# Casts of k and q issued half a pair earlier, first row-maximum pieces in score tiles, and low parts of channel weights shared by GpSimd and VectorE

## The chip, the cores and the metric

One core of a Trainium2 chip runs the whole program. The metric is device time in microseconds (us), the median of several executions. The profile's times count from the start of the profiled span.

## What is computed

The reference runs three stages one after the other. Only the first and the last are touched.

```python
q_pool = q.reshape(B, H, S // 2, 2, D).mean(axis=3)          # 4 x 8 heads, 576 x 64
scores = scale * np.matmul(q_pool, k.transpose(0, 1, 3, 2))  # 576 x 1152
attn = np.exp(scores - np.max(scores, axis=-1, keepdims=True))
attn = attn / (np.sum(attn, axis=-1, keepdims=True) + 1e-09)
x = np.matmul(attn, v)                                       # -> 4 x 576 x 512
...
u, v = relu(x @ w_in), halves                                # gated MLP
x = (u * (w_spatial @ norm(v) + b_spatial)) @ w_out
...
u = x + (x^T @ U @ V)^T                                      # channel MLP
out = u + np.maximum(u @ w_ch1, 0.0) @ w_ch2                 # 512 -> 2048 -> 512
```

The weights of both MLPs arrive as 64-bit floats and are turned into 32-bit ones on the core, then into a rounded high part and a low part (the rest), so that three rounded matmuls stand in for an exact one.

## The kernel before

**Attention.** The 32 heads are worked in 16 pairs; a pair fills the 128 partitions with two heads. A pair has two halves of query columns, 256 and 320 wide, and 9 chunks of 128 keys for each, so 18 chunks, taken in 9 groups of two (`r` is the group's number in its pair, 0 to 8, `i` the group's number in all). A group's work on TensorE is `scores` (L214), `less` (L223, which takes off the row maximum), then `pv` of the group before (L250). ScalarE turns scores into exponentials (`expo`, L234) and GpSimd adds them up (L239). Score tiles come from `ps_s`, which has two buffers.

The row maximum is found beforehand from rounded copies of q and k, in pieces (`piece`, L166 for two heads at once, L163 for the last query columns): one or two matmuls into a PSUM tile `r`, then a reduction on VectorE (L174 or L178) and, after the last piece of a row block, a small minimum (L176, or L184 twice for the last columns). The tile `r` comes from `ring`, which has one buffer, so a piece waits for the reduction of the one before. In each group `some()` issues up to the next piece that is due; by the end of group r = 1 all pieces of the pair itself are done, and the first piece of the next pair stands at the start of group r = 2. `to_rows` turns the maxima of a half into a row (L195, L200 on TensorE, copied by ScalarE at L201 and L206).

The rounded copies are made by ScalarE: `round_k` (L141, one cast of 128x1152) and `round_q` (L130, 128x512, and L135 twice, 64x64). They write one of two buffers (`krs`, `qrs`, `qds`), by the parity of the pair. Before, `round_q(j + 1)` stands at the end of group r = 0 of pair j and `round_k(j + 1)` at the end of r = 1, each behind the exponentials of that group. q itself is pooled by GpSimd (`pool_q`, L124) at the end of r = 4, two pairs ahead.

In the first two groups of the program, one more piece stands behind the scores of each chunk (`if i < 2: some()`), all of them in the one ring buffer.

**Weights.** `Weights.tick` moves one unit of weights (128 x 512 for the channel MLP) through a row of phases, one a tick: two ScalarE passes over the raw words (L493, L494), a clamp and a shift on VectorE (L498, L500), an integer add on GpSimd (L502), a merge on VectorE (L504), the high part on ScalarE (L514) and the low part, a subtraction `do_lo` (L519). Ticks of the gated MLP's weights fall into the attention, one unit every six groups; those of the channel MLP's first ten units fall into the last batch of the gated MLP (table `CFG["END"]`), the other 22 into the first items of the channel MLP. Units alternate: `w1` of block m, `w2` of block m. Before, all 32 low parts run on VectorE.

**Around it.** In the gated MLP's last batch VectorE multiplies (L836), ScalarE and GpSimd split the product (L394, L395), TensorE makes `py` (L860), VectorE takes its low part (L395, tile `yh`), and TensorE's `pU` (L846) needs that. The channel MLP then begins with transposes (L1052), `ph` (L1060) and `py` (L1074).

The order on each engine is the order of the code (the schedule is manual); engines run their queues in order.

Of the kernel before, what the change touches and what calls it, by code (L numbers as in the profile page):

```python
# [10 lines left out]
F32 = mybir.dt.float32  # L11
F32R = mybir.dt.float32r
ACTF = mybir.ActivationFunctionType
ALU = mybir.AluOpType
AX = mybir.AxisListType
# [16 lines left out]
def attention(tc, idf, q, k, v, xs, rounded, also):  # L32
# [13 lines left out]
    nc = tc.nc  # L46
    NP, D, _, _, T = q.shape
# [15 lines left out]
    with ExitStack() as ctx, ExitStack() as sco:  # L63
# [62 lines left out]
        def round_q(j, c0=0, c1=T):  # L126
            s = st[j]
            if "qr" not in s:
                s["qr"] = qrs[j % 2]
            nc.scalar.copy(s["qr"][:, c0:min(c1, 512)], s["q"][:, c0:min(c1, 512)])  # L130
            if c1 == T:
                s["qd"] = qds[j % 2]
                for e in range(2):
                    p = slice(D * e, D * e + D)
                    nc.scalar.copy(s["qd"][p, D * e:D * e + D], s["q"][p, 512:T])  # L135

        def round_k(j, c0=0, c1=S):
            s = st[j]
            if "kr" not in s:
                s["kr"] = krs[j % 2]  # L140
            nc.scalar.copy(s["kr"][:, c0:c1], s["k"][:, c0:c1])  # L141
# [12 lines left out]
        done = [0]  # L154

        def piece(r=None):
            u, c, i, at = pieces[done[0]]
            done[0] += 1
            s, q0 = st[u // 2], HALF[u % 2][2][c]
            r = ring("r") if r is None else r  # L160
            for h, k0 in enumerate(at):
                if c == 2:
                    nc.tensor.matmul(r[:, h, 0:PW], s["qd"], s["kr"][:, k0:k0 + PW], start=True, stop=True)  # L163
                for e in range(2 if c < 2 else 0):
                    p = slice(D * e, D * e + D)
                    nc.tensor.matmul(  # L166
                        r[:, e, 0:PW], s["qr"][p, q0:q0 + 128], s["kr"][p, k0:k0 + PW], start=True, stop=True
                    )
            if i == 0:
                jobs[u]["m"] = ld.tile([128, 2, NPC], F32, tag="m", name="m", bufs=4)  # L170
            m = jobs[u]["m"]
            t = tops[u // 2 % 2][c + 2 * (u % 2)].rearrange("p (e d) -> p e d", e=2)[:, :, 0]
            if c < 2:
                nc.vector.tensor_reduce(out=m[:, :, i], in_=r[:, :, 0:PW], axis=AX.X, op=ALU.max, negate=True)  # L174
                if i == NPC - 1:
                    nc.vector.tensor_reduce(out=t, in_=m, axis=AX.X, op=ALU.min)  # L176
            else:
                nc.vector.tensor_reduce(  # L178
                    out=m[:, 0, i:i + 1], in_=r[:, 0:len(at), 0:PW], axis=AX.XY, op=ALU.max, negate=True
                )  # L180
                if i:
                    for e in range(2):
                        p = slice(D * e, D * e + D)
                        nc.vector.tensor_tensor(out=t[p, e:e + 1], in0=m[p, 0, 0:1], in1=m[p, 0, 1:2], op=ALU.min)  # L184

        def to_rows(u):

            h = u % 2
            n = HALF[h][1]
            t = jobs[u]["top"] = ld.tile([128, NMAX], F32R, tag="toprow", name="toprow")  # L190
            rs = ring("tr")
            for c in range(2):
                for i in range(2):
                    p = slice(64 * i, 64 * i + 64)
                    nc.tensor.matmul(  # L195
                        rs[:, i, 64 * c:64 * c + 64], tops[u // 2 % 2][c + 2 * h][p], idr[p],
                        start=True, stop=True,
                    )
            if h:
                nc.tensor.matmul(rs[:, 0, 128:192], tops[u // 2 % 2][4], idr, start=True, stop=True)  # L200
            nc.scalar.copy(  # L201
                t[:, 0:256].rearrange("p (c i x) -> p i c x", c=2, i=2),
                rs[:, :, 0:128].rearrange("p i (c x) -> p i c x", c=2),
            )
            if h:
                nc.scalar.copy(t[:, 256:n], rs[:, 0, 128:192])  # L206
# [100 lines left out]
        pool_q(1, nc.gpsimd)  # L307
        busy(6)
        to_rows(0)
        chunks = [(u, c) for u in range(NJ) for c in range(KC)]  # L310
        groups = [chunks[i:i + G] for i in range(0, len(chunks), G)]
        PG = 2 * KC // G
# [11 lines left out]
        for i, group in enumerate(groups):  # L324
            j, r = divmod(i, PG)
            if r == 0:
                if j + 2 < NP:
                    load_k(j + 2)
                    load_q(j + 2)
                if j + 1 < NP:  # L330
                    load_v(j + 1)

            end = min(upto[1] + AHEAD + upto[2] * (i + 1) // PG, upto[NJ])

            def some():
                if done[0] < end:
                    piece()

            new = [u for u, c in (groups[i + 1] if i + 1 < len(groups) else ()) if c == 0]
            for u in new:  # L340
                while done[0] < upto[u + 1]:
                    piece()
                to_rows(u)
            if not new:
                some()
            for x in smalls.pop((i, 0), ()):
                x()
            for u, c in group:
                scores(u, c)
                if i < 2:  # L350
                    some()
            last = jobs[group[-1][0]]["s", group[-1][1]]
            for u, c in group:
                less(u, c)
                expo(u, c)
            some()
            for x in smalls.pop((i, 1), ()):
                x()
            if i + 1 == len(groups):
                break  # L360
            for x in before:
                pv(*x)
            before = group

            if i in sums_at:
                sums(sums_at[i], last, NMAX)
            also(i)
            if r == 4 and j + 2 < NP:
                pool_q(j + 2, nc.gpsimd)
            if r == 0 and j + 1 < NP:  # L370
                round_q(j + 1)
            if r == 1 and j + 1 < NP:
                round_k(j + 1)
        sco.close()
        for x in before:
            pv(*x)
# [607 lines left out]
def channel_mlp(tc, ctx, idf, w1, w2, us, out):  # L984
# [4 lines left out]
    nc = tc.nc  # L989
# [27 lines left out]
    for m in range(KM):  # L1017
        src = w1[:, 128 * m:128 * m + 128].rearrange("(k p) f -> p k f", p=128)
        units.append(
            ([(slice(None), src)], 128, (KD, 128))  # L1020
            + parts(
                nc, lambda m=m: [w1s[m][:, 0]], lambda m=m: [w1s[m][:, 1]],
                lambda st: st.rearrange("p (k f) -> p k f", k=KD), nc.vector,
            )
        )
        units.append(
            ([(slice(None), w2[128 * m:128 * m + 128])], 128, (DM,))
            + parts(nc, lambda m=m: [w2s[m][:, 0]], lambda m=m: [w2s[m][:, 1]], eng=nc.vector)
        )

    un, ut, py = {}, {}, {}
# [180 lines left out]
```

## Time and profile before

| | |
|---|---|
| median of 3 runs | 1183.41 us (1182.99 to 1185.17) |
| the profiled execution | 1184.43 us, its span 1182.7 us |
| attention, to the first matmul of the gated MLP | about 515 us |
| gated MLP | about 515 to 757 us |
| channel MLP | about 757 to 1183 us |

Engines' busy time is an average over three stages of different make; the places where TensorE stands still are what the change can act on. In a timeline row the first column is the start, the second the time from the first start to the last end, and the bracket gives the idle time of that engine before it and what ended it.

### The profile page before, as it was taken

Reading aid. Unit: us, or ns where it says so; the run is one execution under the profiler, and the core shown is the slowest. Engines: PE = TensorE matmul, PEld = TensorE weight load, DVE = VectorE, ACT = ScalarE, POOL = GpSimd, SP = SyncE. Lnnn points to the kernel's source line nnn. Section 1 sums busy time; section 2 is a strip of 40 time slices with the busy share of each in tenths; the row PEclk is TensorE's granted clock in tenths of the full one; section 3 lists DMA queues with packets and bytes.
Section 4 is the critical chain, followed back from the end, with each engine's and each line's share of the span. In section 5 each row is a group of like instructions: output and inputs, shape, how many; then the busy total and the mean of one; then the engine's idle time right before and its main releaser. Section 6 shows DMA issues by size and latency. Waiting matters only on the chain.

```text
span 1182.7 us, 18287 instructions
## 1 busy us (share of the span) xinstructions
PE 1135.9 (96%) x7242; PEld 887.0 (75%) x7242; DVE 616.7 (52%) x967; ACT 446.6 (38%) x877; POOL 566.4 (48%) x467
## 2 busy tenths in 40 slices
PE   7999999999999999999999999799999999999998
PEld 5655556655655555669898988689999999999997
DVE  4576777766787777544333336888822112121211
ACT  2455555455545555444333334555411111111110
POOL 2789999988889988843242436353300000000000
PEclk7899999999999999999999999899999999999999
DMA  7122333333334320011020106343202001010000
GB/s 213 27 82 82 94 89 91 81 81 99 88 106 115 82 81 31 17 51 54 1 81 10 41 2 221 120 147 125 90 27 81 1 1 54 1 54 1 27 1 27
DMA packets 37768, 79.18 MB, mean 67 GB/s; under 512 B 5553, under 2 KB 17841, under 8 KB 37682
## 3 DMA queue, kind: packets, MB, share of 16 engines
q1 hardware_dynamic: 37682, 78.01, 21.9%
q8 instruction: 57, 0.93, 0.3%
q14 instruction: 29, 0.24, 0.1%
HBM read 63.31 MB, written 14.16 MB: 66 GB/s over the span
## 4 chain that ended last, share of the span: by engine, by line
PE 80%; DVE 10%; ACT 4%; issue 3%; DMA 1%; POOL 1%; SPq 0%; ACTq 0%; DVEq 0%; POOLq 0%
PE ph L1060 17%; PE py L1074 17%; PE s L214 10%; PE po L250 8%; DVE m L174 5%; PE r L166 4%; PE pu L812 4%; PE pv L677 4%; PE pg L830 4%; PE py L860 3%; PE s L223 2%; ACT pt L234 2%; PE s L263 2%; DVE sum L275 2%; ACT yh L141 1%
## 5 line engine op out<-in xcount | busy, mean ns | idle before, releaser
L239 POOL TENSOR_TENSOR acc<-acc,pt 128x512 f32<-128x512 f32 (+1 forms) x222 | 316.9, 1427 | 59.0 <-ACT pt L234 47.4
L234 ACT ACTIVATE pt<-s 128x512 f32<-128x512 f32 (+1 forms) x288 | 171.7, 648 | 211.9 <-PE s L223 202.3
L174 DVE TENSOR_REDUCE m<-r 128x2 f32<-128x768 f32 x192 | 182.5, 952 | 90.8 <-PE r L166 88.1
L1074 PE MATMUL py<-w,h 128*128 128x512 f32 x864 | 218.4, 397 | 1.9 <-ACT h L1063 1.4
L1060 PE MATMUL ph<-ut,w 128*128 128x384 f32 x1152 | 218.4, 338 | 0.0
L1060 PEld LDWEIGHTS ph<-ut,w 128*128 128x128 f32 x1152 | 205.5, 188 | 8.5
L1064 DVE SCALAR_TENSOR_TENSOR h<-ph,h 128x384 fp32r<-128x384 f32 x96 | 53.5, 557 | 267.1 <-ACT h L1063 267.0
L1074 PEld LDWEIGHTS py<-w,h 128*128 128x128 f32 x864 | 160.5, 189 | 32.6 <-ACT h L1063 1.7
L250 PE MATMUL po<-pt,v 128*64 128x320 f32 (+1 forms) x1152 | 172.3, 420 | 0.0
L214 PE MATMUL s<-q,k 64*128 64x320 f32 (+1 forms) x1152 | 170.2, 414 | 0.0
L1063 ACT ACTIVATE h<-ph 128x384 fp32r<-128x384 f32 x96 | 47.2, 492 | 310.8 <-PE ph L1060 310.8
L214 PEld LDWEIGHTS s<-q,k 64*128 64x128 f32 x1152 | 105.2, 188 | 21.0 <-ACT yh L135 3.5
L250 PEld LDWEIGHTS po<-pt,v 128*64 128x64 f32 x1152 | 70.1, 136 | 55.5 <-issue 24.8
L166 PE MATMUL r<-yh 64*128 64x384 f32 x384 | 81.4, 422 | 23.8 <-ACT yh L141 12.3
L275 DVE RECIPROCAL sum<-sum 128x64 f32<-128x64 f32 (+1 forms) x128 | 75.0, 591 | 55.5 <-ACT sum L268 55.5
L166 PEld LDWEIGHTS r<-yh 64*128 64x128 f32 x384 | 36.6, 188 | 77.5 <-DVE m L174 45.3
L502 POOL TENSOR_TENSOR st<-st,raw 128x512 int32<-128x512 int32 (+3 forms) x48 | 69.0, 1439 | 53.0 <-DVE st L500 45.2
L223 PE MATMUL s<-toprow,yh 64*128 64x256 f32 (+1 forms) x576 | 93.3, 402 | 0.0
L223 PEld LDWEIGHTS s<-toprow,yh 64*128 64x128 f32 x576 | 55.4, 189 | 16.1 <-issue 0.4
L830 PE MATMUL pg<-wst,vn 128*128 128x288 f32 x448 | 60.1, 295 | 0.0
L830 PEld LDWEIGHTS pg<-wst,vn 128*128 128x128 f32 x448 | 59.6, 188 | 0.0
L812 PEld LDWEIGHTS pu<-xt,wi 128*128 128x128 f32 x384 | 53.3, 188 | 2.1
(120 smaller groups left out, 1206.5 us busy)
## 6 DMA issues: line engine op xcount, KB each, us to landing
raw<-in_moe_w_ch_dram SPq DMA_DIRECT2D x32, 512.0 KB, 3.7
k<-in_k_dram SPq DMA_DIRECT2D x32, 288.0 KB, 4.4
qraw<-in_q_dram SPq DMA_DIRECT2D x32, 288.0 KB, 5.7
v<-in_v_dram SPq DMA_DIRECT2D x16, 576.0 KB, 5.0
xn<-x SPq DMA_DIRECT2D x4, 1152.0 KB, 5.4
out_dram<-un SPq DMA_DIRECT2D x18, 256.0 KB, 2.1
raw<-in_moe_w_in_dram SPq DMA_DIRECT2D x8, 512.0 KB, 4.1
u<-o SPq DMA_DIRECT2D x16, 256.0 KB, 2.0
```

The source lines that it names most:

```text
L166: nc.tensor.matmul(r[:, e, 0:PW], s["qr"][p, q0:q0 + 128], s["kr"][p, k0:k0 + PW], start=True, stop=True)
L174: nc.vector.tensor_reduce(out=m[:, :, i], in_=r[:, :, 0:PW], axis=AX.X, op=ALU.max, negate=True)
L214: nc.tensor.matmul(t[:, e, 0:n], s["k"][p, 128 * c:128 * c + 128], s["q"][p, q0:q0 + n], start=True, stop=False)
L223: nc.tensor.matmul(jb["s", c][:, e, 0:n], first[p], jb["top"][p, 0:n], start=False, stop=True)
L234: nc.scalar.activation(x[:, :, 0:n], t[:, :, 0:n], ACTF.Exp, scale=SC)
L239: nc.gpsimd.tensor_tensor(out=a, in0=jb["p", 0][:, :, 0:n] if c == 1 else a, in1=x[:, :, 0:n], op=ALU.add)
L250: nc.tensor.matmul(jb["o"][D * e:D * e + D, 0:n], st[u // 2]["v"][:, e, c], x[:, e, 0:n], start=c == 0, stop=c == KC - 1,)
L275: nc.vector.reciprocal(out=t, in_=t)
L812: nc.tensor.matmul(p[:, 0:HT], wi[0][:, a, k, 128 * m:128 * m + 128], xt[:, c, k, HT * h:HT * h + HT], start=i == 0, stop=i == 3 * KD - 1,)
L830: nc.tensor.matmul(p[:, 0:HT], vn[:, a, s, 128 * m:128 * m + 128], wst[:, c, s, sl], start=s == 0 and i == 0, stop=s == NT - 1 and i == 1,)
L1060: nc.tensor.matmul(p[:, 0:BT], w1s[m][:, a, k], ut[i][:, c, k], start=j == 0, stop=j == 3 * KD - 1)
L1074: nc.tensor.matmul(py[i][c], h[:, a, 128 * c:128 * c + 128], w2s[m][:, e], start=m == 0 and a + e == 0, stop=m == KM - 1 and a == 1,)
```

## The change

Four edits. (1) `round_k(j + 2)` now stands at the end of group r = 5 of pair j and `round_q(j + 2)` at the end of r = 6; those of pair 1 stand ahead of the first group. (2) In the first two groups the extra pieces no longer stand between the scores: up to two follow the exponentials of the group, each in a score tile (`r1`, from `ps_s`). (3) The small minimum of the last columns is a reduction over two values, not a two-input minimum. (4) The low parts of the channel weights: w1 of blocks 0 to 4 and all of w2 go to GpSimd, w1 of blocks 5 to 15 stay on VectorE.

```diff
-                        nc.vector.tensor_tensor(out=t[p, e:e + 1], in0=m[p, 0, 0:1], in1=m[p, 0, 1:2], op=ALU.min)
+                        nc.vector.tensor_reduce(out=t[p, e:e + 1], in_=m[p, 0, 0:2], axis=AX.X, op=ALU.min)
...
         to_rows(0)
+        round_q(1)
+        round_k(1)
...
                 scores(u, c)
-                if i < 2:
-                    some()
...
                 expo(u, c)
             some()
+
+            for _ in range(2 if i < 2 else 0):
+                if done[0] < end:
+                    piece(ps_s.tile([128, 2, 512], F32, tag="s", name="r1"))
...
-            if r == 0 and j + 1 < NP:
-                round_q(j + 1)
-            if r == 1 and j + 1 < NP:
-                round_k(j + 1)
+
+            if r == 6 and j + 2 < NP:
+                round_q(j + 2)
+            if r == 5 and j + 2 < NP:
+                round_k(j + 2)
...
-                lambda st: st.rearrange("p (k f) -> p k f", k=KD), nc.vector,
+                lambda st: st.rearrange("p (k f) -> p k f", k=KD), nc.gpsimd if m < 5 else nc.vector,
...
-            + parts(nc, lambda m=m: [w2s[m][:, 0]], lambda m=m: [w2s[m][:, 1]], eng=nc.vector)
+            + parts(nc, lambda m=m: [w2s[m][:, 0]], lambda m=m: [w2s[m][:, 1]])
```

Lines behind the first edit are 1 to 5 higher in the changed kernel (L493 to L519 become L498 to L524, L395 becomes L400, L889 becomes L894).

**ScalarE in a pair.** Before, from the 640-wide exponentials of one pair through the 512-wide ones of the next (`yh` is the room of all rounded copies):

```order
L234 ACTIVATE pt<-s 128x640 x2
L234 ACTIVATE pt<-s 128x2x256 x2
L130 CAST yh<-q 128x512
L135 CAST yh<-q 64x64 x2
L234 ACTIVATE pt<-s 128x2x256 x2
L141 CAST yh<-k 128x1152
L234 ACTIVATE pt<-s 128x2x256 x2
L268 ACTIVATE sum<-s 128x320
```

Now, from the group that also carries weights:

```order
L498 ACTIVATE st_99<-raw_96 128x512
L499 ACTIVATE raw_96<-raw_96 128x512
L519 CAST wi_94<-st_98 128x512
L141 CAST yh<-k 128x1152
L234 ACTIVATE pt<-s 128x640 x2
L130 CAST yh<-q 128x512
L135 CAST yh<-q 64x64 x2
L234 ACTIVATE pt<-s 128x640 x2
L268 ACTIVATE sum<-s 128x256
L201 CAST toprow<-tr 128x2x2x64
L234 ACTIVATE pt<-s 128x640 x2
L234 ACTIVATE pt<-s 128x2x256 x6
```

Both casts moved from the 512-wide half of the next pair to the 640-wide half of the pair before; three groups of exponentials now follow each other with no cast between.

**TensorE at the first two groups.** Before, from the first row of maxima on (numbers tell the tiles apart):

```order
L166 MATMUL r_278<-yh_80 128x384 x2
L214 MATMUL s_283<-q_203,k_144 128x256 x2
L166 MATMUL r_286<-yh_80 128x384 x2
L214 MATMUL s_290<-q_203,k_144 128x256 x2
L166 MATMUL r_293<-yh_80 128x384 x2
L223 MATMUL s_283<-toprow_263,yh_80 128x256 x2
L223 MATMUL s_290<-toprow_263,yh_80 128x256 x2
L166 MATMUL r_308<-yh_80 128x384 x2
L166 MATMUL r_316<-yh_80 128x384 x2
L214 MATMUL s_320<-q_203,k_144 128x256 x2
```

Now:

```order
L166 MATMUL r_282<-yh_80 128x384 x2
L214 MATMUL s_287<-q_203,k_144 128x256 x2
L214 MATMUL s_290<-q_203,k_144 128x256 x2
L223 MATMUL s_287<-toprow_263,yh_80 128x256 x2
L223 MATMUL s_290<-toprow_263,yh_80 128x256 x2
L166 MATMUL r_303<-yh_80 128x384 x2
L166 MATMUL r1_307<-yh_80 128x384 x2
L166 MATMUL r1_312<-yh_80 128x384 x2
L166 MATMUL r_317<-yh_80 128x384 x2
L214 MATMUL s_321<-q_203,k_144 128x256 x2
```

The same pieces are there; two of a group's four now take score tiles, and the scores of a group stand together.

**GpSimd in the last batch of the gated MLP.** Before, from the third block's product (`gt`, `gtt`) to the last of the ten units (`st` is the staged unit):

```order
L395 TENSOR_TENSOR gt_5564<-ut_5359,gt_5564 128x288
L502 TENSOR_TENSOR st0_7079<-st0_7079,raw0_7098 128x512
L395 TENSOR_TENSOR gt_5564<-ut_5359,gt_5564 128x224
L395 TENSOR_TENSOR gtt_5565<-ut_5359,gtt_5565 128x64
L502 TENSOR_TENSOR st1_7080<-st1_7080,raw1_7099 128x512
L502 TENSOR_TENSOR st2_7081<-st2_7081,raw2_7100 128x512
L502 TENSOR_TENSOR st3_7082<-st3_7082,raw3_7101 128x512
L502 TENSOR_TENSOR st0_7079<-st0_7079,raw0_7098 128x512
L502 TENSOR_TENSOR st1_7080<-st1_7080,raw1_7099 128x512
```

Now:

```order
L400 TENSOR_TENSOR gt_5564<-ut_5359,gt_5564 128x288
L524 TENSOR_TENSOR w1_1_7087<-st2_7081,w1_1_7087 128x512
L507 TENSOR_TENSOR st0_7079<-st0_7079,raw0_7098 128x512
L400 TENSOR_TENSOR gt_5564<-ut_5359,gt_5564 128x224
L400 TENSOR_TENSOR gtt_5565<-ut_5359,gtt_5565 128x64
L524 TENSOR_TENSOR w2_1_7088<-st3_7082,w2_1_7088 128x512
L507 TENSOR_TENSOR st1_7080<-st1_7080,raw1_7099 128x512
L524 TENSOR_TENSOR w1_2_7089<-st0_7079,w1_2_7089 128x512
L507 TENSOR_TENSOR st2_7081<-st2_7081,raw2_7100 128x512
L524 TENSOR_TENSOR w2_2_7090<-st1_7080,w2_2_7090 128x512
L507 TENSOR_TENSOR st3_7082<-st3_7082,raw3_7101 128x512
```

Between each two integer adds there is now a low part; eight of the first ten stand ahead of the tenth unit's integer add.

## Rows read from the trace of the kernel before

**Rows 1.** The page: busy time of each engine, share of the span.

```profile
PE 1135.9 (96%) x7242; PEld 887.0 (75%) x7242; DVE 616.7 (52%) x967; ACT 446.6 (38%) x877; POOL 566.4 (48%) x467
```

**Rows 2.** Waits, whole span: who waited for whom, us, times, longest.

```profile
PE r L166 <- ACT yh L141: 12.3, 15, 2.0
```

**Rows 3.** Timeline of one pair without weights on ScalarE.

```profile
217.15 0.56 DVE L178 TENSOR_REDUCE m<-r 128x1 f32<-128x384 f32 x1 [0.39 <-PE r L163]
...
217.75 1.42 DVE L184 TENSOR_TENSOR yh<-m 64x1 fp32r<-64x1 f32 x2
217.83 1.15 ACT L141 CAST yh<-k 128x1152 fp32r<-128x1152 f32 x1
...
219.03 0.44 PE L166 MATMUL r<-yh 64*128 64x384 f32 x2 [0.91 <-ACT yh L141]
...
225.15 2.62 POOL L239 TENSOR_TENSOR acc<-acc,pt 128x512 f32<-128x512 f32 x2 [1.23 <-ACT pt L234]
...
230.19 1.41 POOL L124 TENSOR_TENSOR q<-qraw 128x576 f32<-128x576 f32 x1
...
233.55 1.30 ACT L234 ACTIVATE pt<-s 128x640 f32<-128x640 f32 x2 [1.74 <-PE s L223]
```

**Rows 4.** Timeline of group r = 5 in a pair with weights.

```profile
138.73 0.68 ACT L493 ACTIVATE st<-raw 128x512 f32<-128x512 f32 x1
...
139.86 0.62 ACT L514 CAST wi<-st 128x512 fp32r<-128x512 f32 x1
...
141.10 1.30 ACT L234 ACTIVATE pt<-s 128x640 f32<-128x640 f32 x2 [0.62 <-PE s L223]
...
142.59 1.24 PE L214 MATMUL s<-q,k 64*128 64x320 f32 x8
```

**Rows 5.** Timeline of the program's first groups.

```profile
18.78 0.37 ACT L201 CAST toprow<-tr 128x256 fp32r<-128x256 f32 x1 [7.73 <-PE tr L195]
...
20.70 0.44 PE L166 MATMUL r<-yh 64*128 64x384 f32 x2 [0.62 <-DVE m L174]
...
23.16 1.09 ACT L234 ACTIVATE pt<-s 128x512 f32<-128x512 f32 x2 [4.01 <-PE s L223]
...
24.27 0.62 ACT L130 CAST yh<-q 128x512 fp32r<-128x512 f32 x1
...
24.80 0.49 ACT L135 CAST yh<-q 64x64 fp32r<-64x64 f32 x2
...
25.68 0.69 PE L166 MATMUL r<-yh 64*128 64x384 f32 x2 [1.05 <-DVE m L174]
...
33.75 0.69 PE L166 MATMUL r<-yh 64*128 64x384 f32 x2
```

**Rows 6.** Windows: stretch, length, busy of each engine, TensorE's granted clock, DMA.

```profile
21.00:22.00 1.00, 0.57 (x6) 0.17 (x2) 0.82 (x1) 0.00 (x0) 0.00 (x0) 0.97 1.02 408
...
35.00:36.00 1.00, 1.00 (x10) 0.76 (x6) 0.44 (x1) 0.00 (x0) 0.00 (x0) 0.70 0.00 0
```

**Rows 7.** Timeline of the gated MLP's end, where channel weights are staged.

```profile
747.45 0.69 DVE L504 SCALAR_TENSOR_TENSOR st<-raw,st 128x512 int32<-128x512 int32 x1
...
747.67 1.64 POOL L502 TENSOR_TENSOR st<-st,raw 128x512 int32<-128x512 int32 x1 [1.48 <-DVE st L500]
...
748.05 1.80 DVE L519 TENSOR_TENSOR w<-st,w 128x512 fp32r<-128x512 f32 x1
...
751.38 1.63 POOL L502 TENSOR_TENSOR st<-st,raw 128x512 int32<-128x512 int32 x1 [2.08 <-DVE st L500]
...
757.31 0.79 PE L846 MATMUL pU<-yh,uu 128*128 128x512 f32 x1 [3.77 <-DVE yh L395]
...
758.98 0.68 DVE L519 TENSOR_TENSOR w<-st,w 128x512 fp32r<-128x512 f32 x1
...
759.11 1.12 PE L1052 MATMUL pt<-idf,un 128*128 128x128 f32 x4 [1.01 <-DVE yh L395]
```

**Rows 8.** Timeline, early channel MLP.

```profile
785.01 0.73 PE L1074 MATMUL py<-w,h 128*128 128x512 f32 x2 [1.41 <-ACT h L1063]
```

## The prediction

> **What bounds the kernel now.** I read the page's busy times first: TensorE's matmuls fill 1135.9 of 1182.7 us [rows 1], so at most 46.8 us of standing still can be won, plus what a lower clock costs. No other engine is near its limit over the whole span. So the question is only at which places TensorE waits, for whom, and whether the change takes that wait away. The view of waits and then the timeline, stretch by stretch, give three places that the change touches.
>
> The first is once in a pair: the first row-maximum piece of the next pair waits for the cast of k. The waits come to 12.3 us, 15 of them, and the longest, 2.0, is the very first cast of the program at its start, which stays [rows 2]. So 12.3 - 2.0 = 10.3 us lie in 14 pairs, 0.7 a pair. The timeline shows one: the cast runs from 217.83 to 218.98 and the piece starts at 219.03, after 0.91 us of idle [rows 3].
>
> The second is the program's beginning: pieces follow each other through one PSUM buffer, each waiting for VectorE's reduction of the one before, with idle times of 0.62 to 1.05 us [rows 5]. The clock granted to TensorE falls there from full speed, 2.4 GHz, to half, 1.2 GHz, about 22 us in, after a stretch in which matmuls filled 0.57 of a window, and comes back at about 35 us, after stretches without a pause [rows 6].
>
> The third is the end of the gated MLP, where VectorE and GpSimd stage channel weights and TensorE waits 3.77 and 1.01 us for VectorE's low part of `yh` [rows 7], and shortly afterwards 1.41 us for a ScalarE result that stands in the same queue as the weights [rows 8].
>
> **Edit 1, the casts.** Nothing is added or removed: 15 casts of k and of q stand elsewhere. What is late next, once the piece needn't wait? It needs the ring buffer, which the reduction before it leaves at 217.15 + 0.56 = 217.71 [rows 3], and TensorE itself is busy until 219.03 - 0.91 = 218.12. So the piece can start then, and the whole 0.91 us goes. GpSimd, the engine nearest to its limit in this stage, waits 1.23 us for exponentials behind that point [rows 3], so it can follow a pair that is 0.91 us shorter. I take 10.0 of the 10.3 us.
>
> The cover in the new place is ScalarE's idle time. Before the exponentials that follow group r = 5 it stands idle 1.74 us [rows 3], and the cast of k takes 1.15, so 0.59 is left. The cast of q (0.62 + 0.49 = 1.11 [rows 5]) comes a group later, into an idle time of the same kind. It needs q pooled by GpSimd, which was done at 230.19 + 1.41 = 231.60, while the exponentials of its group end at 233.55 + 1.30 = 234.85 [rows 3]: 3.2 us to spare. Every second pair has weights on ScalarE at the end of r = 5, which leave only 0.62 us [rows 4]; there the cast overruns by 1.15 - 0.62 = 0.53 us. Who waits for that? TensorE's next scores at 142.59 need the first of the two exponentials gone from its tile, now at 141.10 + 0.53 + 0.65 = 142.28 [rows 4], so 0.31 us are left and nothing is lost. If that cover is gone, a pair pays what the delay exceeds. No DMA moves, and no queue but ScalarE's changes.
>
> **Edit 2, the first groups.** Casts for pair 1 now stand ahead of the first exponentials: the row copy ends at 19.15, then 0.62 + 0.49 + 1.15 = 2.26 us of casts, so the exponentials run from 21.4 to 22.5 instead of from 23.16 [rows 5]. Score tiles come free for the extra pieces at 22.0 and 22.5. Reductions, 0.96 us each, can now follow each other, since four of the eight pieces no longer share the ring's buffer. Followed through by hand with the rows' durations at full clock, the first piece of the third group starts at about 28.4; with the slow clock all along (0.69 a piece instead of 0.44 [rows 5], the rest alike), at about 31.4. It was at 33.75 [rows 5]. That is a gain of 5.3 or 2.4 us; I take 4, since TensorE has fewer pauses but still some, and keep 2.3 and 6 (the latter with the slow matmuls from 33.75 to 35.4 at full speed too) as ends.
>
> **Edit 3, the small minimum.** Two of them took 1.42 us on VectorE [rows 3]; no TensorE wait hangs on them, since the next reduction begins only behind the piece that waited. I take 0, ends 0 and -1 us.
>
> **Edit 4, the low parts.** VectorE is rid of 21 subtractions. One took 1.80 us while GpSimd's integer add ran, and 0.68 with none beside it [rows 7]. The rows show why: the add began at 747.67, was held until VectorE's merge ended at 748.14, and ended at 749.31; the subtraction, begun at 748.05, ended at 749.85, 0.54 us after it. The two engines take turns, the second standing still until the first is through. So an add holds what they share for 749.31 - 748.14 = 1.17 us, a VectorE subtraction for 0.54. The Trainium skill, SBUF — State Buffer, section Who interferes with whom, says that the first to issue has the shared ports for the whole instruction and the other "fully blocks". By that rule, which this row bears out, moving a subtraction lengthens the shared time; if the ports were merely split, VectorE's queue would be shorter by some 1.1 us or more a unit, and the two TensorE waits of 3.77 and 1.01 us would go.
>
> On GpSimd the subtraction takes a turn of 1.17 us for one of 0.54, so 0.63 us more for each unit. Eight of them now stand ahead of the tenth integer add, on which hang VectorE's merge, its low part of `yh` and TensorE's last `pU`: 8 x 0.63 = 5.0 us at most. Units are 751.38 - 747.67 = 3.71 us apart [rows 7]; the turns in it (1.17, 0.54, 0.55 for the merge, and a clamp and a shift) leave some of it free, which takes part of the 5.0. On the other side, if VectorE's shorter queue decides, the 3.77 + 1.01 us go, and with the clock's recovery perhaps 11 us in all (these waits, two earlier ones of about 4 us and the half-speed matmuls behind them; an estimate). I take +2 us, nearest to the first case, because the rows show the turns to be exact; ends -4 and +5 for the likeliest case. In the first channel items VectorE loses every second subtraction, which stood ahead of `h`; of the 1.41 us [rows 8] I take 1 off, ends -3 and +1. Later TensorE never waits, and nothing is won.
>
> **The sum.** -10.0 - 4 + 0 + 2 - 1 = -13 us. Against the profiled execution, 1184.43 us, that is 1171.4. This execution stood 1.0 above the median of the runs, so 1170.4 is to be compared with 1183.41.
>
> **Rivals.** (a) *VectorE's relief pays in full*: the waits at the end of the gated MLP vanish, -11 and -3 instead of +2 and -1: 1170.4 - 15 = 1155. For it: the waits name VectorE; against it: the turns in [rows 7]. (b) *The turns cost more and the casts return half*: -5 - 2.3 + 5 + 1 = -1.3, 1182. It needs GpSimd, more loaded in the last pairs, to hold back exponentials once TensorE is faster; against it stands its idle 1.23 us a pair [rows 3]. (c) *The piece still waits*: if its wait is bound to ScalarE's queue rather than to the cast it reads, the 10 us stay and 1180.4 comes out; the order shows the cast some five groups earlier, which speaks against it. (d) *Slower*: ScalarE's idle time doesn't cover the casts. Both sit in front of exponentials now; from the point where the delay passes 0.53 + 0.31 = 0.84 us (the spare in [rows 4]) the two score buffers are not free and TensorE waits. Were none of the 1.15 + 1.11 us covered in the 14 pairs, it would pay 14 x 2.26 = 32 us and win 10 back: 1170.4 + 32 = 1202; the exponentials' idle of 1.74 us [rows 3] speaks against it.
>
> **How the numbers follow.** The forecast, with its terms between their ends, has 0.81; (a) 0.07, (b) 0.06, (c) 0.03, (d) 0.03. The ends of the terms, not all at once, give 1163 to 1178; (a), (b), (c) and (d), 0.19 together, lie outside. About 0.2% (2.4 us) is what a measurement of this kernel can tell from no change. Faster: 0.81 + 0.07 + 0.03 from (c) and half of (b), 0.94. Same: the other half of (b), 0.03. Slower: (d), 0.03.
>
> **What the next profile would show.** If right: no wait of `r` for the cast of k but the first one; a pair without weights some 0.9 us shorter; the third group's first piece at 28 to 31 us; TensorE's attention end about 14 us earlier; GpSimd busy longer by some 27 us, VectorE shorter by 30 or more; the wait ahead of the channel MLP's first transposes as long as before or longer. Wrong it would be if exponentials at r = 6 or 7 waited for casts, if `s` waited for `pt`, or if the stage from the gate's last matmul to the first transposes shrank by several us.

## The result, and the profile after

The changed kernel takes 1168.28 us in the median of four runs (1167.35 to 1169.9), the kernel before beside it 1183.72 (1182.99 to 1185.17): ratio 0.987, 95% interval 0.9852 to 0.9887. Forecast were 1170.4 us and a range of 1163 to 1178. The profiled execution took 1167.6 us with a span of 1165.8, against 1184.43 and 1182.7 before.

The page's busy line answers to [rows 1]:

```profile
PE 1129.8 (97%) x7242; PEld 884.7 (76%) x7242; DVE 585.6 (50%) x946; ACT 446.4 (38%) x877; POOL 597.5 (51%) x488
```

VectorE does 31 us less, GpSimd 31 us more, ScalarE the same. TensorE's standing still fell from 46.8 to 1165.8 - 1129.8 = 36.0 us, which is 10.8 of the 16.9 us between the spans; the other 6.1 are in its busy time, 1129.8 against 1135.9 for the same 7242 matmuls; the mean granted clock of the profiled execution rose from 0.985 to 0.992 of full speed. Two rows of what is left, from the view of waits of the changed kernel (who waited for whom, us, times, longest):

```profile
PE py L865 <- POOL gt L400: 2.2, 2, 1.5
...
PE r L166 <- ACT yh L141: 0.7, 1, 0.7
```

Fifteen waits for the cast of k [rows 2] have become one, the first of the program. At the gated MLP's end new ones stand beside the old: TensorE waits 2.2 us there for GpSimd's part of the product, `gt`, where it was 0.5. To see what each place gave, I cut every profiled execution at four marks of its timeline: the first row copy (ScalarE, `toprow`), the first sums and the last sums in a score tile (TensorE, L263 on `s`), and the channel MLP's first transposes (`pt`). For the changed kernel and the kernel before, those marks are these rows (start, length):

```profile
17.10 0.37 ACT L201 CAST toprow<-tr 128x256 fp32r<-128x256 f32 x1 [6.04 <-PE tr L195]
...
44.88 0.66 PE L263 MATMUL s<-acc,ones 128*64 128x128 f32 x8
...
491.02 0.66 PE L263 MATMUL s<-acc,ones 128*64 128x128 f32 x8 [0.17 <-ACT pt L234]
...
743.49 2.82 PE L1057 MATMUL pt<-idf,un 128*128 128x128 f32 x12 [2.42 <-DVE yh L400]
```

```profile
52.53 0.66 PE L263 MATMUL s<-acc,ones 128*64 128x128 f32 x8
...
509.79 0.66 PE L263 MATMUL s<-acc,ones 128*64 128x128 f32 x8 [0.17 <-ACT pt L234]
```

The stages between them, in us, one profiled execution each (the last column ends with the span; the rows below the difference are of the experiments told further down):

| kernel | to the row copy | to the first sums | to the last sums | to the transposes | to the end | span |
|---|---|---|---|---|---|---|
| before | 18.78 | 33.75 | 457.26 | 249.32 | 423.59 | 1182.7 |
| changed | 17.10 | 27.78 | 446.14 | 252.47 | 422.31 | 1165.8 |
| difference | -1.68 | -5.97 | -11.12 | +3.15 | -1.28 | -16.9 |
| edit 1 alone | 17.15 | 33.67 | 446.07 | 249.37 | 424.04 | 1170.3 |
| edit 2 alone | 17.22 | 26.68 | 457.10 | 249.39 | 423.41 | 1173.8 |
| edit 4 undone | 18.61 | 28.93 | 446.14 | 249.89 | 423.03 | 1166.6 |
| edit 4 only behind the first ten units | 17.23 | 27.02 | 446.12 | 249.87 | 421.66 | 1161.9 |
| the same, first ten without low parts | 17.47 | 27.04 | 446.09 | 243.47 | 421.33 | 1155.4 |
| cast of k twice | 19.01 | 27.99 | 451.85 | 252.75 | 422.00 | 1173.6 |
| no integer add, low parts on VectorE | 18.57 | 27.89 | 446.51 | 244.77 | 420.36 | 1158.1 |
| no integer add, low parts on GpSimd | 17.20 | 27.04 | 446.50 | 247.50 | 420.66 | 1158.9 |
| before, longer warm-up | 17.04 | 33.47 | 457.11 | 249.96 | 423.12 | 1180.7 |
| edit 4 only behind the first ten units, longer warm-up | 17.10 | 29.65 | 446.18 | 250.14 | 421.33 | 1164.4 |

So the casts gave 11.1 us, the first groups 6.0, the low parts cost 3.2 and gave 1.3 back, and 1.7 us came ahead of anything that the change touches. The table also says how far one execution can be trusted: in the stage up to the transposes, the kernel before and the same kernel with a longer warm-up, equal there, differ by 0.64 us, and in the last stage the five kernels with all low parts on VectorE and the add on GpSimd differ by 1.0.

**The pair.** Timeline of the changed kernel at the boundary that answers to [rows 3], and the casts in their new place a pair earlier:

```profile
192.11 1.17 ACT L141 CAST yh<-k 128x1152 fp32r<-128x1152 f32 x1
...
206.35 1.08 PE L250 MATMUL po<-pt,v 128*64 128x256 f32 x8
...
207.36 0.45 PE L166 MATMUL r<-yh 64*128 64x384 f32 x2
...
210.12 0.76 PE L263 MATMUL s<-acc,ones 128*64 128x160 f32 x8 [0.20 <-ACT pt L234]
...
239.15 0.76 PE L263 MATMUL s<-acc,ones 128*64 128x160 f32 x8 [0.20 <-ACT pt L234]
```

The piece at 207.36 waits for nothing. It even begins 0.07 us before the modelled end of the matmuls ahead of it (206.35 + 1.08 = 207.43), as matmuls without a stall between them do. From the sums behind this boundary to those behind the next, 239.15 - 210.12 = 29.03 us go by. The same stretch before, with the next boundary's wait in it:

```profile
221.79 0.76 PE L263 MATMUL s<-acc,ones 128*64 128x160 f32 x8 [0.20 <-ACT pt L234]
...
249.04 0.44 PE L166 MATMUL r<-yh 64*128 64x384 f32 x2 [0.91 <-ACT yh L141]
...
251.80 0.76 PE L263 MATMUL s<-acc,ones 128*64 128x160 f32 x8 [0.20 <-ACT pt L234]
```

That is 30.01, so the boundary gave 0.98: the idle 0.91 and the 0.07 of overlap that the stall had broken.

**The first groups.** Timeline of the changed kernel's start, which answers to [rows 5]:

```profile
20.59 1.82 DVE L174 TENSOR_REDUCE m<-r 128x2 f32<-128x768 f32 x2 [1.50 <-PE r L166]
...
20.73 1.32 PE L166 MATMUL r<-yh 64*128 64x384 f32 x6 [0.18 <-ACT pt L234]
...
26.99 0.44 PE L166 MATMUL r<-yh 64*128 64x384 f32 x2
```

Three pieces stand together, reductions follow without a gap, and the third group's first piece starts at 26.99, 9.89 us behind the row copy, where it was 33.75 - 18.78 = 14.97. The prediction named 28 to 31 us for it; most of the rest is the row copy's 1.68.

**The gated MLP's end.** Its timeline in the changed kernel answers to [rows 7]:

```profile
732.48 1.68 POOL L507 TENSOR_TENSOR st<-st,raw 128x512 int32<-128x512 int32 x1 [0.36 <-DVE st L505]
...
734.11 1.49 POOL L524 TENSOR_TENSOR w<-st,w 128x512 fp32r<-128x512 f32 x1
...
734.48 1.40 DVE L505 TENSOR_SCALAR st<-st 128x512 int32<-128x512 int32 x1
...
735.80 0.68 DVE L509 SCALAR_TENSOR_TENSOR st<-raw,st 128x512 int32<-128x512 int32 x1
736.01 1.60 POOL L507 TENSOR_TENSOR st<-st,raw 128x512 int32<-128x512 int32 x1 [0.41 <-POOL w L524]
...
736.40 1.50 DVE L503 TENSOR_SCALAR st<-st 128x512 f32<-128x512 f32 x1
...
737.59 1.45 POOL L524 TENSOR_TENSOR w<-st,w 128x512 fp32r<-128x512 f32 x1
...
739.39 1.67 POOL L507 TENSOR_TENSOR st<-st,raw 128x512 int32<-128x512 int32 x1 [0.36 <-DVE st L505]
...
740.57 0.49 PE L851 MATMUL pU<-yh,uu 128*128 128x512 f32 x1 [2.40 <-DMA raw<-in_moe_w_ch_dram]
```

Read the ends, not the starts. The low part on GpSimd ends at 735.60; VectorE's shift, begun at 734.48, ends 0.28 after it, at 735.88. The add ends at 736.01 + 1.60 = 737.61; less its own 1.17 it began in earnest at 736.44, 0.56 after the shift, when the merge was through. The clamp ends at 737.90, 0.29 after the add; the next low part at 739.04, 1.14 after the clamp. So the five operations of a unit follow each other without a gap: 0.28 + 0.56 + 1.17 + 0.29 + 1.14 = 3.44 us, and add follows add at 3.53 (736.01 - 732.48) and 3.38. The shift and the clamp each stand still for a whole GpSimd operation. In the trace of before, with none beside them, they are 0.43 and 0.41 long:

```profile
750.38 0.41 DVE L498 TENSOR_SCALAR st<-st 128x512 f32<-128x512 f32 x1
...
750.82 0.43 DVE L500 TENSOR_SCALAR st<-st 128x512 int32<-128x512 int32 x1
```

(The releaser named at 740.57 is a DMA, but VectorE's operation that writes `yh`, begun at 739.84, ended at 739.84 + 0.68 = 740.52; that is what `pU` waited for.)

The turns are not where the stage got longer. That is earlier, where GpSimd also splits the product (`gt`, `gtt`). GpSimd from the second of the ten adds to the fifth, in the changed kernel, then these two adds in the version with the first ten low parts on VectorE (told below):

```profile
707.40 1.76 POOL L507 TENSOR_TENSOR st<-st,raw 128x512 int32<-128x512 int32 x1
...
711.71 1.29 POOL L524 TENSOR_TENSOR w<-st,w 128x512 fp32r<-128x512 f32 x1
...
716.69 1.26 POOL L524 TENSOR_TENSOR w<-st,w 128x512 fp32r<-128x512 f32 x1
...
720.10 1.73 POOL L524 TENSOR_TENSOR w<-st,w 128x512 fp32r<-128x512 f32 x1
...
721.78 1.47 POOL L507 TENSOR_TENSOR st<-st,raw 128x512 int32<-128x512 int32 x1
```

```profile
706.72 1.75 POOL L507 TENSOR_TENSOR st<-st,raw 128x512 int32<-128x512 int32 x1
...
717.86 1.74 POOL L507 TENSOR_TENSOR st<-st,raw 128x512 int32<-128x512 int32 x1
```

From the second add to the fifth it takes 14.38 us here and 11.14 there; from the fifth to the tenth 739.39 - 721.78 = 17.61 here and 735.62 - 717.86 = 17.76 there. So all of the loss comes between the second and the fifth add, and none in the five units behind. The kernel with the cast of k twice repeats the first of each pair (14.39 and 17.64), the kernel before the second (11.16 and 17.72). In that stretch three low parts stand in GpSimd's queue, and but for 1.1 us at its start in both kernels that queue has no idle time, with them or without. The cause is read off these traces; no run moved the three low parts alone.

### The profile page after: what moved, and what is told of

Read it like the earlier page. It is cut to its first block, busy times and chain, and to the rows that moved or that the text cites. A ratio compares the mean times of both kernels' runs of the same rounds, so it can differ in the third digit from the quotient of the medians.

```text
span 1165.8 us, 18278 instructions
## 1 busy us (share of the span) xinstructions
PE 1129.8 (97%) x7242; PEld 884.7 (76%) x7242; DVE 585.6 (50%) x946; ACT 446.4 (38%) x877; POOL 597.5 (51%) x488
## 4 chain that ended last, share of the span: by engine, by line
PE 80%; DVE 9%; DMA 3%; issue 2%; ACT 2%; POOL 2%; SPq 0%; ACTq 0%; POOLq 0%; DVEq 0%
PE ph L1065 17%; PE py L1079 17%; PE s L214 10%; PE po L250 8%; DVE m L174 5%; PE pu L817 4%; PE pv L682 4%; PE pg L835 4%; PE r L166 4%; PE py L865 3%; PE s L223 2%; PE s L263 2%; DMA qraw<-in_q_dram 2%; DVE sum L275 2%; POOL acc L239 1%
```

## The experiments

**Edit 1 alone**: the kernel before with the casts moved, those of pair 1 in their old place.

```diff
-            if r == 0 and j + 1 < NP:
-                round_q(j + 1)
-            if r == 1 and j + 1 < NP:
-                round_k(j + 1)
+            if r == 6 and j + 2 < NP:
+                round_q(j + 2)
+            if r == 5 and j + 2 < NP:
+                round_k(j + 2)
+            if i == 0:
+                round_q(1)
+            if i == 1:
+                round_k(1)
```

> The kernel before with the first edit alone: casts of k and q for pairs 2 to 15 at the ends of groups r = 5 and r = 6 two pairs ahead, those of pair 1 where they were. Theory (the piece at the pair's boundary waits only for the cast, and ScalarE's idle time covers the casts): the waits of r for the cast of k after the first one go, about 10.3 us, so 1183.4 - 10.3 = 1173 us, ratio 0.991; GpSimd stays even with the shorter pairs. Rival (casts half returned elsewhere, because GpSimd or the exponentials hold back a faster TensorE): 1178, ratio 0.9955. Rival (the edit needs the other three): 1183, ratio 1.000.

Measured: 1172.61 us, ratio 0.9911 (0.9897 to 0.9925), 11.1 less than 1183.74. Behind the row copy, which came 1.6 us earlier, only the stage from first to last sums differs by more than 0.5, 446.07 against 457.26. The theory holds and neither rival does. Edit 3 is not in this kernel: its small minimum still takes 13.7 us on VectorE where the changed kernel's takes 4.8, yet the stage is as long as the changed kernel's 446.14. So edit 3 is worth nothing in that stage.

```profile
L184 DVE TENSOR_TENSOR yh<-m 64x1 fp32r<-64x1 f32 x32 | 13.7, 427 | 0.9
```

```profile
L184 DVE TENSOR_REDUCE yh<-m 64x1 fp32r<-64x2 f32 x32 | 4.8, 150 | 0.9
```

(Groups of instructions, of edit 1 alone and of the changed kernel: busy us, mean ns, idle before.)

**Edit 2 alone**: the kernel before with the extra pieces behind the exponentials.

```diff
                 scores(u, c)
-                if i < 2:
-                    some()
...
             some()
+            for _ in range(2 if i < 2 else 0):
+                if done[0] < end:
+                    piece(ps_s.tile([128, 2, 512], F32, tag="s", name="r1"))
```

> The kernel before with the second edit alone: the extra pieces of the first two groups behind the exponentials, in score tiles; all casts where they were. Theory (four of eight pieces leave the one ring buffer, reductions follow each other, TensorE is back at full clock sooner): the third group's first piece at 27 to 29 us instead of 33.75, 5 to 6 us saved, 1177.5 to 1178.5 us, ratio 0.9955. Rival (the gain of the changed kernel's start came from the early casts, or from the clock in the warm-up): less than 2 us, 1182, ratio 0.999.

Measured: 1176.77 us, ratio 0.994 (0.9928 to 0.9953), 7.0 less. From row copy to first sums 26.68 against 33.75: 7.1 us, a little more than in the changed kernel (27.78), where the clock still fell to half from 17.7 to 21.1 us. Here it stayed up. The third group's first piece starts at 26.03, earlier than the 27 to 29 expected. The gain is this edit's own, not the early casts'. Nor is it the clock's in the warm-up: edit 1 alone and the kernel before with a longer warm-up had full speed at the row copy too, fell to half at about 20 us and took 33.67 and 33.47.

**Edit 4 undone, and edit 4 behind the first ten units only.** Both start from the changed kernel.

```diff
-                lambda st: st.rearrange("p (k f) -> p k f", k=KD), nc.gpsimd if m < 5 else nc.vector,
+                lambda st: st.rearrange("p (k f) -> p k f", k=KD), nc.vector,
...
-            + parts(nc, lambda m=m: [w2s[m][:, 0]], lambda m=m: [w2s[m][:, 1]])
+            + parts(nc, lambda m=m: [w2s[m][:, 0]], lambda m=m: [w2s[m][:, 1]], eng=nc.vector)
```

In the second, the last line ends in `eng=nc.vector if m < 5 else nc.gpsimd`.

> The changed kernel with the fourth edit undone: all 32 low parts on VectorE again. Theory (in the trace of the changed kernel the gated MLP's end takes 3.15 us more and the early channel MLP 1.28 us less, both from this edit, because a low part on GpSimd takes a longer turn): 1168.3 - 1.9 = 1166.4 us, ratio 0.9855. Rival (VectorE's relief pays, and the 3.15 us are from an earlier start that meets its DMA or clock otherwise): 1168 or more, ratio 0.987 to 0.99.

> The changed kernel with the low parts of blocks 0 to 4 (staged in the gated MLP's end) on VectorE as before, and those of w2 of the later blocks on GpSimd as in the changed kernel. Theory (the loss lies in the first ten units, the gain in the later ones): both at their best, 1168.3 - 3.2 = 1165.1 us, ratio 0.9845. Rival (the gain of the channel MLP's beginning came from the first ten units, staged otherwise): 1166.4, as with all of them on VectorE, ratio 0.9855.

Measured: undone 1167.94 us, ratio 0.9864 (0.9851 to 0.9878); behind the first ten only 1164.53, ratio 0.9843 (0.9829 to 0.9857). By its time the first missed the expected 1166.4: it stands 0.3 us from the changed kernel, within the spread of either, as the rival had it. Its profiled execution began with the slow row copy at 18.61. The stages tell more: with the first ten low parts on VectorE, the way from last sums to transposes takes 249.9 in both, not 252.5; with the later w2 ones on GpSimd the last stage takes 421.7 instead of 423.0. So edit 4 costs 2.6 us in the gated MLP's end and gives about 1 back behind it (the last stage took 421.3 to 422.3 in the five kernels that share the later low parts and have the add on GpSimd, 423.0 to 424.0 in the five that have all low parts on VectorE). The other 0.6 of the 3.2 in the table lies ahead of the first of the ten adds, where executions of equal code differ by as much. The version that keeps the half that gains came out as expected, 3.75 us below the changed kernel.

**No low parts in the first ten units.** From the version just told; low parts are set to zero once, ahead of the last batch (w1's by GpSimd, w2's by VectorE), so the part of the result that they carry is missing.

```diff
-            u["lo"](u["st"])
+            if u["lo"]:
+                u["lo"](u["st"])
...
+    units[:10] = [x[:4] + (None,) for x in units[:10]]
```

> As the version with the first ten low parts on VectorE and the later w2 ones on GpSimd (1164.5 us), but the ten low parts of blocks 0 to 4 are left out (their room is set to zero once, ahead of the last batch), so the part of the result that they carry is missing. Theory (a low part costs by the turn that it takes of what VectorE and GpSimd share; on GpSimd eight of them, 0.63 us longer each, cost 2.6 us of the stage from the last sums to the first transposes): without their turns of 0.54 us the stage is 8 x 0.54 x 2.6 / 5.0 = 2 to 3 us shorter than 249.9. Rival (it is the length of VectorE's queue, 1.2 to 1.8 us a low part, that the last pU waits for): the waits of 3.8, 1.0 and 1.0 us at the stage's end vanish, and the stage is 6 us shorter or more, with the clock's recovery up to 9.

Measured: 1157.78 us, ratio 0.9781 (0.9766 to 0.9796); the stage takes 243.47, 6.4 us less. That is the rival's figure. About 0.5 of it lies ahead of the first of the ten adds, where executions of equal code differ by as much. My conversion of turns into time was wrong: a low part on VectorE costs about 0.6 us in the mean of the ten, not a share of its turn. Timelines of the version with low parts on VectorE, then of this one:

```profile
728.79 1.64 POOL L507 TENSOR_TENSOR st<-st,raw 128x512 int32<-128x512 int32 x1 [1.48 <-DVE st L505]
...
732.51 1.63 POOL L507 TENSOR_TENSOR st<-st,raw 128x512 int32<-128x512 int32 x1 [2.08 <-DVE st L505]
732.90 1.80 DVE L524 TENSOR_TENSOR w<-st,w 128x512 fp32r<-128x512 f32 x1
...
735.62 1.61 POOL L507 TENSOR_TENSOR st<-st,raw 128x512 int32<-128x512 int32 x1 [1.48 <-issue]
```

```profile
726.03 1.64 POOL L508 TENSOR_TENSOR st<-st,raw 128x512 int32<-128x512 int32 x1 [0.88 <-DVE st L506]
726.42 0.68 DVE L400 TENSOR_TENSOR yh<-py,yh 128x512 fp32r<-128x512 f32 x1
...
728.56 1.64 POOL L508 TENSOR_TENSOR st<-st,raw 128x512 int32<-128x512 int32 x1 [0.88 <-DVE st L506]
728.94 1.53 DVE L504 TENSOR_SCALAR st<-st 128x512 f32<-128x512 f32 x1
```

Add follows add at 3.72 (with an operation of `yh` between) and 3.11 us with low parts on VectorE, at 2.53 without (with a `yh`), at 3.53 (with a `yh`) and 3.38 with them on GpSimd. VectorE stands still for the add's 1.17 us in the low part (1.80) or, where there is none and no `yh` stands ahead of it, in the clamp (1.53); a `yh`, which takes one input from PSUM, runs its 0.68 us beside the add (726.42). So with low parts on VectorE the unit is VectorE's chain, in which GpSimd waits 1.5 to 2.1 us for the next shift; with them on GpSimd it is the 3.44 us of turns without a gap. The move changed the bound of these late units and hardly their length, 3.4 us in the mean of two either way.

**Six more matmuls in the warm-up**, in the version with edit 4 only behind the first ten units and in the kernel before (`WARM = 50` for 44).

> The version with the first ten low parts on VectorE and the later w2 ones on GpSimd (1164.5 us), with 50 matmuls in the warm-up instead of 44. Theory (executions differ by whether TensorE's clock falls at 12 us; it fell where the warm-up ended at 8.4 or 8.6 us and not where it ended at 9.1 or later, and a fall there costs 1.5 us up to the first row copy and some more behind it): every execution then starts as the faster ones do, the first row copy at 17.1 to 17.3 us, the median 1163.5 to 1164, and the spread of the runs below 2 us. Rival (the clock falls for another reason): median and spread as they were, 1164.5.

> The kernel before with 50 matmuls in the warm-up instead of 44 and nothing else. Theory (the clock's fall at 12 us comes with the idle time of 1.8 to 2 us between warm-up and first piece): first row copy at 17.2 us in place of 18.78, median 1182.5 to 1183 (most runs of before started well already), ratio 0.999. Rival: no difference, 1183.7.

Measured: 1165.11 us (1164.45 to 1166.31), ratio 0.9841 (0.9828 to 0.9855); and 1182.82, ratio 0.9992 (0.9983 to 1.0001). Both profiled executions began well, row copy at 17.10 and 17.04, and the spread of the first fell from 4.0 to 1.9 us, but the first median is 0.6 us higher than without, not lower as expected, and the second 0.9 lower with an interval that reaches 1. In the first the clock fell at 23 us instead, and the way to the first sums took 29.65. Inconclusive as a gain.

**The cast of k twice**, in the changed kernel.

```diff
                 round_k(j + 2)
+                round_k(j + 2)
```

> The changed kernel with the cast of k at the end of r = 5 made twice (14 more casts of 1.15 us on ScalarE). Theory (ScalarE's idle time covers the casts, and a delay of the next exponentials costs only what passes 0.84 us): pairs without weights have 0.7 to 1.5 us of idle left there and pay nothing; in the seven pairs with weights the exponentials come 1.68 us late instead of 0.53, 0.84 us over the spare, so 7 x 0.84 = 6 us more than the changed kernel, 1174 us, ratio 0.992. Rival 1 (nothing covers it, each cast costs its whole length): 14 x 1.15 = 16 us, 1184. Rival 2 (the spare is larger, for instance because a late group is caught up): 1168.3, ratio 0.987.

Measured: 1173.74 us, ratio 0.9912 (0.9897 to 0.9926), 5.5 over the changed kernel; the stage from first to last sums takes 451.85, 5.7 more. Pairs without weights lose at most 0.04 us, six with weights 0.69 to 1.13, a seventh 0.33. The timeline of one of the six:

```profile
133.91 2.34 ACT L141 CAST yh<-k 128x1152 fp32r<-128x1152 f32 x2
...
136.16 1.29 ACT L234 ACTIVATE pt<-s 128x640 f32<-128x640 f32 x2
...
136.91 1.40 PE L214 MATMUL s<-q,k 64*128 64x320 f32 x8 [0.63 <-ACT pt L234]
```

TensorE waits for the first of the two exponentials, the step that the prediction put 0.31 us of spare on. The theory holds, within half a microsecond of its sum.

**No integer add.** ScalarE's pass rounds the low word down, so that one VectorE operation shifts and sets the bits; all units. On the version with the first ten low parts on VectorE, and on the changed kernel.

```diff
-            nc.scalar.activation(lo, lo.bitcast(U32), ACTF.Copy, scale=2.0**-29)
+            nc.scalar.activation(lo, lo.bitcast(U32), ACTF.Copy, scale=(1 - 2.0**-20) * 2.0**-29, bias=-0.5)
...
-                nc.vector.tensor_scalar(out=o, in0=o, scalar1=3, scalar2=None, op0=ALU.logical_shift_left)
+                pass
             elif phase == 3:
-                nc.gpsimd.tensor_tensor(out=o, in0=o, in1=lo, op=ALU.add)
+                nc.vector.scalar_tensor_tensor(
+                    out=o, in0=o, scalar=3, in1=lo, op0=ALU.logical_shift_left, op1=ALU.bitwise_or
+                )
```

> The version with the first ten low parts on VectorE and the later w2 ones on GpSimd (1164.5 us), with the integer add on GpSimd taken out: ScalarE's pass rounds the low word down to 0 to 7, so that one VectorE operation shifts and sets these bits, in place of VectorE's shift and GpSimd's add. All 48 weight units are staged so. Theory (the stage's unit of 3.1 to 3.7 us is VectorE's chain of clamp, shift, add by GpSimd, merge and low part; without the add's turn of 1.17 us it is 0.4 + 0.6 + 0.6 + 0.6 = 2.2, with yh 2.8): 0.9 us a unit over nine units, the stage from last sums to first transposes 6 to 9 us shorter than 249.9, and 1 us more in the channel MLP's beginning: 1164.5 - 8 = 1156.5 us, ratio 0.977. Rival 1 (ScalarE or the weights' DMA sets the unit next): 3 us shorter, 1161.5. Rival 2 (VectorE's two-input operations are no shorter without GpSimd beside them): no gain, 1164.5.

> The changed kernel (low parts of w1 of blocks 0 to 4 and of all w2 on GpSimd) with the same fused operation in place of VectorE's shift and GpSimd's add. Theory (in the changed kernel the unit of 3.46 us is the sum of the turns, 1.17 + 1.17 + 0.28 + 0.28 + 0.55 = 3.45; with the add out it is 1.17 + 0.28 + 0.55 + 0.55 = 2.55 of shared time, no better than VectorE's chain of 2.2 to 2.8): about as fast as the version with these low parts on VectorE, 1156 to 1159 us, ratio 0.978. Rival (with the add gone GpSimd is free and VectorE's relief pays in full): 3 us or more faster than that version.

Measured: low parts on VectorE 1157.81 us, ratio 0.9778 (0.9765 to 0.9791); on GpSimd 1161.78, ratio 0.981 (0.9797 to 0.9824). The stage takes 244.77 and 247.50. The timeline of the first, then of the second:

```profile
728.13 0.69 DVE L511 SCALAR_TENSOR_TENSOR st<-raw,st 128x512 int32<-128x512 int32 x1
...
730.27 0.68 DVE L507 SCALAR_TENSOR_TENSOR st<-st,raw 128x512 int32<-128x512 int32 x1
...
730.99 0.69 DVE L511 SCALAR_TENSOR_TENSOR st<-raw,st 128x512 int32<-128x512 int32 x1
```

```profile
729.46 1.36 POOL L526 TENSOR_TENSOR w<-st,w 128x512 fp32r<-128x512 f32 x1 [1.28 <-ACT w L521]
729.58 1.79 DVE L507 SCALAR_TENSOR_TENSOR st<-st,raw 128x512 int32<-128x512 int32 x1
```

Without GpSimd beside them VectorE's operations take 0.69 us, the unit with a `yh` 730.99 - 728.13 = 2.86, and the stage is 5.1 us shorter, less than the 6 to 9 expected. Where low parts run on GpSimd, the fused operation takes 1.79, as the low part did beside the add, and the stage is 2.7 longer, so the second missed its 1156 to 1159, and its rival came no nearer. The price is as large as with the add in place, but it does not come from a full queue: GpSimd stands idle 1.28 us ahead of the low part shown, and the merges fall behind by 1.3 us from the second to the fifth and by 1.6 from there to the tenth. Here the turns cost. The first of the two is 10.5 us faster than the changed kernel, the best that was run with all its work.

## Why the prediction was right, and where it was off

- **Edit 1**, forecast -10.0: right in place and mechanism, measured -11.1 in the stage of the changed kernel and in the median of edit 1 alone. The idle rows were taken at their face; each stall also breaks an overlap of 0.07 us, 14 times, which makes up the difference. GpSimd followed the shorter pair, as its idle 1.23 us said, and rivals (b) for the casts, (c) and (d) did not come.
- **The cover**: the overrun of 0.53 us in pairs with weights cost nothing, and with the cast doubled the 0.84 us of spare decided as computed.
- **Edit 2**, forecast -4 with an end of -6: measured -6.0 (-7.1 alone). The replay by hand was right in its steps and some 0.8 us long: at full clock it had the third group's piece 28.4 - 18.78 = 9.6 us behind the row copy, and edit 2 alone, at full clock all along, has it at 26.03 - 17.22 = 8.81. That the changed kernel's 9.89 lies so near to 9.6 is luck, since its clock was at half for 3.4 us. The step that was off was "I take 4": the middle between two clocks, where the clock came back at 21.1 us already.
- **Edit 3**, forecast 0: right in the stage from first to last sums, by the comparison with edit 1 alone.
- **Edit 4**, forecast +2 and -1: +2.6 and about -1 by the stages with edit 4 undone. Rival (a) did not come. The Trainium skill, SBUF — State Buffer, section Who interferes with whom, as cited in the prediction, says that whichever of the two engines issues first has the shared ports for its whole instruction. The trace agrees: the chain of ends above is one engine at a time, and without GpSimd's operation VectorE's 1.8 us are 0.7. What the prediction had wrong is hidden in a sum that came out well: it charged the difference of two turns, 0.63 us, to each of eight units. The traces put the whole loss, 3.2 us at the fifth add, where three low parts went into a GpSimd queue without idle time, and nothing on the late units, whose turns are the bound only with low parts on GpSimd; on VectorE they are VectorE's chain, in which a low part costs about 0.6 us. That +2 stands so near to +2.6 is luck.
- **Not in the sum**: 1.7 us ahead of the row copy. The sum was made against a profiled execution in which the clock fell early, and the changed kernel's did not. The 1.0 us taken off for a slow execution covers a part of it.

Against the terms of the sum the stages moved by -1.1 (casts), -2.0 (first groups), +1.2 and -0.3 (low parts), so a part of the nearness of 1170.4 to 1168.28 is errors that cancel. Medians of single edits do not add up exactly: -11.1 for the casts, -7.0 for the first groups and 1168.28 - 1167.94 = +0.3 for the low parts make -17.8, against the -15.4 between the medians. The clock's fall at the changed kernel's start, which edit 2 alone did not have, accounts for about 1 us of the 2.4 (27.78 against 26.68); executions of one kernel here lie 1.9 to 4.1 us apart.

## What to carry to other kernels

Where two engines take turns at a resource, add up the turns of one unit and, beside it, the chain of the engine that waits and the whole queue of the engine that takes an operation over, in each stretch by itself: moving an operation helps only where that queue has idle time and the turns leave room, and here taking a turn away (the add) was worth more than moving one. A short wait in a queue that must not wait can be removed by moving its producer to where that engine idles; the idle time ahead of the next consumer, plus that consumer's own spare, says how much fits. Before a difference between two kernels is read, cut both traces at the same marks: a stage that the change doesn't touch shows how much the executions differ by themselves.

## What the runs showed of the hardware that was not expected

TensorE's clock at 12 us differs from execution to execution of equal code. Windows of the kernel before, then of the changed kernel (length, busy of each engine, then the granted clock, third from the end):

```profile
12.00:13.00 1.00, 1.00 (x5) 0.67 (x6) 1.00 (x2) 0.00 (x0) 0.38 (x1) 0.50 0.97 194
```

```profile
12.00:13.00 1.00, 1.00 (x8) 0.65 (x8) 1.00 (x2) 0.00 (x0) 0.39 (x1) 1.00 0.95 217
```

Up to there both run the same instructions. In the four profiled executions whose warm-up matmuls ended at 8.3 to 8.8 us, TensorE then stood idle for 1.7 to 2.4 us, the clock fell to 1.2 GHz and the row copy came at 18.6 to 19.0. In the six others with the same 44 they ended at 9.1 to 9.7, the idle time was 0.7 to 1.5 us, the clock stayed at 2.4 GHz there and the row copy came at 17.1 to 17.5. The 44 begin at 2.0 us in all ten, and end earlier where they run faster earlier. The windows show it, before and then in the changed kernel (the number behind the first busy share counts matmuls):

```profile
5.00:6.00 1.00, 1.00 (x12) 1.00 (x10) 0.00 (x0) 0.00 (x0) 0.00 (x0) 1.00 1.09 230
```

```profile
5.00:6.00 1.00, 1.00 (x7) 1.00 (x6) 0.00 (x0) 0.00 (x0) 0.00 (x0) 1.00 0.97 230
```

Twelve a microsecond is the pace that all reach. From 5 to 6 us the four run 9 to 12, the six 7; the changed kernel's reaches 12 only from 8 to 9 us. An earlier speed-up thus ends the warm-up earlier, leaves a longer idle time behind it, and in the four executions with the longest the clock falls. Why the speed-up comes at different times stays open, and the two runs with a longer warm-up don't show that lengthening it pays.
